# A first tile multiplied plainly, weight conversions in steps, and 12 early chunks: one change to a one-core attention and feed-forward kernel

## The chip, the core and the metric

The kernel runs on one core of one Trainium2 chip. Five engines take part, each with its own instruction stream that it works off strictly in order: TensorE (PE in the rows; its weight loads are PEld), VectorE (DVE), ScalarE (ACT), GpSimd (POOL) and SyncE (SP), which only issues transfers here. The metric is the device time of one execution in microseconds; less is better. The kernel before took 2212.39 us (median of 3 runs, 2211.89 to 2212.9).

## The reference

Channel attention, then a feed-forward network with a leaky activation. B = 4, N = 6080, C = 256, d_ff = 2048.

```python
qn = q / (np.linalg.norm(q, axis=1, keepdims=True) + 1e-06)
kn = k / (np.linalg.norm(k, axis=1, keepdims=True) + 1e-06)
s = kn.transpose(0, 2, 1) @ qn / tau          # 256 x 256 for each batch
s = s - s.max(-1, keepdims=True)
a = np.exp(s)
a /= a.sum(-1, keepdims=True) + 1e-09
x = v @ a                                     # then all batches as one list of 24320 tokens
h = x @ w_in                                  # 256 -> 2048
g = np.maximum(0.01 * h, h)
out = g @ w_out                               # 2048 -> 256
```

q, k and v are float32; w_in and w_out come as float64.

## The kernel before, in words

**The algebra.** For each batch the kernel computes the 256x256 attention matrix `a`, multiplies it into w_in once (W = a·w_in) and then needs only two products for each token: h = v·W and out = g·w_out. Every factor is kept as a high half (rounded to the fast float32 format of TensorE) and a low half (the rest), and a product is three passes: high·high, low·high, high·low.

**Batch matrices.** q and k come in 48 chunks of 128 rows, two chunks to a group. Batch 0 is worked off at the start in plain float32: ACT squares a group, DVE adds the squares up, PE multiplies (each plain float32 matmul shows as two records, so a chunk is 4 records of 256 columns). The chunks of the next batch are cast and multiplied in three passes (6 matmuls of 256 columns) in the gaps of the main loop. Batch 1 is an exception: its first FILL = 12 groups (24 chunks) are multiplied plainly during the start, where TensorE would wait for the norms, the softmax and the turn of `a`; only their squares are left for the loop ("quick" chunks).

**The main loop.** 24 tiles of 1024 tokens (6 for each batch, the last of a batch 960), and for each tile 8 pairs `p` of channel blocks: 192 steps, numbered w. In each pair h = v·W is a product of 2x2 blocks by Strassen's method (Winograd's form): 7 block products of 3 matmuls of 512 columns, `block_product`, into the PSUM banks x, y and z. ACT copies an intermediate out of its bank (`taken`), DVE adds the other bank (`add`), and `leaky` makes of each of the four results C11, C22, C21, C12 a `g_split` tile: ACT Prelu, ACT cast (high half), DVE subtract (low half). `ffn_out` then issues 24 matmuls of g·w_out, one pair later, in portions (`out(5)`, `out(5)`, `out(8)`, the rest).

**Weights.** w_in and w_out are converted from float64 words by ACT and DVE, 512 columns a block (`f64_split`, L320: two ACT steps, five DVE steps, an ACT cast for the high half, a DVE subtract for the low half). Half of w_in is converted during the chunks of batch 0, the rest and w_out in `convert` steps at the head of pairs 0 to 5. For each of 4 column groups j, `w_product` (12 matmuls for its two halves h) makes W, and `w_parts` makes of it Strassen's 7 block factors, their high and low halves, for two pairs. They go to `w_dram` and are read again for each tile (`w_load`); for batch 0 the halves are made on the tile `w_split` itself, and the whole tile is stored.

**What sets the order.** Three things. The program order, written out in the main loop. Queues (`todo`): `put` appends an entry with an estimated length to the queue of an engine, and `slot(queue, room)` at a fixed place of a pair takes entries from its head as long as they fit. And `in_order`, which ties an instruction behind the last one of its engine that was issued this way; what is not tied (the conversions, the plain products of the chunks, the chain of the start) is placed by a scheduler that follows its own estimate of time. Buffers rotate by tag: w_split 4, v_split 10, g_split 5, temp 8, raw 4 (loads of float64 words, of q and k, and of w_in halves), w_first and w_rest 1 each.

Of the kernel before, what the change touches and what calls it, by code (L numbers as in the profile page):

```python
# [11 lines left out]
I32 = mybir.dt.int32  # L12
# [9 lines left out]
EARLY_LOAD = (12, 14, 16, 18)  # L22
EARLY_SPLIT = (17, 19, 21, 23)
FILL = 12
# [7 lines left out]
def channel_attention_ffn(  # L32
# [287 lines left out]
    def f64_split(raw, hi, lo):  # L320
        low, high = raw[:, :, 0], raw[:, :, 1]
        scale, x = temp(I32, "f64_scale"), temp(I32, "f64_x")
        nc.vector.tensor_scalar(
            out=scale, in0=high, scalar1=20, scalar2=0x7FF, op0=ALU.logical_shift_right, op1=ALU.bitwise_and
        )
        nc.vector.tensor_scalar(out=x, in0=high, scalar1=0xFFFFF, scalar2=None, op0=ALU.bitwise_and)
        nc.scalar.activation(out=scale, in_=scale, func=AF.Relu, bias=exp_bias[:, 0:1], scale=2.0**23)
        tail = low.bitcast(F32)
        nc.scalar.activation(out=tail, in_=low.bitcast(U32), func=AF.Copy, scale=2.0**-52)
        nc.vector.scalar_tensor_tensor(  # L330
            out=scale, in0=high, scalar=-(2**31), in1=scale, op0=ALU.bitwise_and, op1=ALU.bitwise_or
        )
        x32 = x.bitcast(F32)
        nc.vector.scalar_tensor_tensor(out=x32, in0=x, scalar=2.0**-20, in1=tail, op0=ALU.mult, op1=ALU.add)  # L334
        nc.vector.scalar_tensor_tensor(
            out=x32, in0=x32, scalar=1.0, in1=scale.bitcast(F32), op0=ALU.add, op1=ALU.mult
        )
        nc.scalar.copy(out=hi, in_=x32)
        nc.vector.tensor_tensor(out=lo, in0=x32, in1=f32(hi), op=ALU.subtract)

    class Conversions:


        def __init__(self, blocks):
            self.blocks, self.loaded = list(blocks), []

        def load(self):
            bits, split = self.blocks.pop(0)
            self.loaded.append((f64_load(bits), split))
# [9 lines left out]
    def win_tile(early):  # L359
        if early:  # L360
            return work.tile([P, 2, TW], F32R, name="win_early", tag="v_split", bufs=VBUFS)
        return ld.tile([P, 2, TW], F32R, name="win", tag="raw", bufs=RBUFS)
# [4 lines left out]
    def win_block(j, h, early):  # L367
        def split(raw):
            w = win[j, h] = win_tile(early)
            f64_split(raw, w[:, 0, :], w[:, 1, :])  # L370
            nc.sync.dma_start(out=win_dram[j][h], in_=flat(w))

        return w_in[h * P:(h + 1) * P, j * TW:(j + 1) * TW], split

    def win_load(j):
        for h in range(CH):
            win[j, h] = win_tile(False)
            nc.sync.dma_start(out=flat(win[j, h]), in_=win_dram[j][h])
# [16 lines left out]
    def w_product(b, j, h, tag):  # L395
# [8 lines left out]
        return last  # L404

# [11 lines left out]
    def w_parts(b, j):  # L417
# [25 lines left out]
        for k in range(2):  # L443
            p, w = 2 * j + k, []

            def blocks(x0, n, name, k=k, w=w, p=p):

                if b == 0:
                    return [w_split[0, p][:, x, x0:x0 + n, :] for x in range(2)]
                w.append(work.tile([P, 2, n, P], F32R, name=name, bufs=1))  # L450
                return [w[-1][:, x] for x in range(2)]

            def store(x0, n, w=w, p=p):
                if b:
                    nc.sync.dma_start(
                        out=w_dram[b, p][:, :, x0 * P:(x0 + n) * P],
                        in_=f32(w[-1].rearrange("p x s f -> p x (s f)")),
                    )

            def begin(k=k, p=p, blocks=blocks, store=store):  # L460
                if b == 0:
                    w_split[0, p] = w_tile()
# [5 lines left out]
            def rest(k=k, p=p, blocks=blocks, store=store):  # L468
                last = split(k, blocks(S1, 4, "w_rest"), S1, (s12, S1, 2), (s34, S3, 2))
                store(S1, 4)  # L470
                if b == 0:
                    w = w_split[0, p]
                    nc.sync.dma_start(
                        out=w_dram[0, p].rearrange("p x f -> p (x f)"), in_=f32(w.rearrange("p x s f -> p (x s f)"))
                    )
                return last

            yield 1.0, begin
            yield 1.2, rest
# [11 lines left out]
    def wo_block(i):  # L491
        fs = slice(i * FPB, (i + 1) * FPB)

        def split(raw):
            f64_split(raw, *(wo[x][:, fs, :].rearrange("p f d -> p (f d)") for x in range(2)))

        return w_out.rearrange("(f p) d -> p f d", p=P)[:, fs, :], split
# [22 lines left out]
    def v_parts(i):  # L520
# [4 lines left out]
        t2 = temp(name="v_t2")[:, 0:w]  # L525
# [4 lines left out]
        yield 1.1, lambda: v_split_of(i, "B11", b11)  # L530
        yield 1.1, lambda: v_split_of(i, "B21", b21)
# [4 lines left out]
        yield 1.1, lambda: v_split_of(i, "T2", t2)  # L536
        yield 1.1, lambda: v_split_of(i, "T1", b11)
# [382 lines left out]
```

## Time and profile before

| what | value |
|---|---|
| time, median of 3 runs | 2212.39 us |
| profiled execution: time, span | 2212.01 us, 2210.1 us |
| PE busy, share of the span | 2169.7 us, 98% |
| DVE busy, ACT busy | 1472.3 us (67%), 1487.3 us (67%) |
| PE busy 0 to 50 us (chunks of batch 0) | 45.02 us |
| PE busy 50 to 85.5 us (norms, softmax, early chunks) | 29.29 us of 35.5 |
| PE busy 85.5 to 203 us (first tile) | 95.60 us of 117.5, granted clock 0.93 |
| PE busy 203 to 300 us (second tile) | 97.00 us of 97.0, granted clock 1.00 |

Rows of a timeline give the start, the time from first start to last end, engine, line, operation, tiles written and read, shape and count; in square brackets stands the idle time of the engine before, and what ended it. Rows of a group give the count, the total busy time and the mean of one in ns. A matmul's record is longer than its turn: records overlap, so the turn is read from the starts.

### The profile page before, as it was taken

The page shows a single profiled execution, that of the slowest core. Times are in us where ns is not written, and L with a number is a line of the kernel's source. Part 1 is how long each engine was busy: PE and PEld are TensorE (multiplying, and loading weights), DVE is VectorE, ACT ScalarE, POOL GpSimd, SP SyncE. Part 2 cuts the span into 40 slices and gives each one's busy share as a digit, 9 for nine tenths or more (in the row PEclk, how much of TensorE's full clock was granted, in tenths as well). Part 3 has the DMA queues.
Part 4 walks back from the last instruction along what each step waited for, and adds up shares of the span by engine and source line. Part 5 has one row for each costly group of instructions (what it writes and reads, how often), then busy time and mean ns, then how long its engine had stood idle before and what let it go on. Part 6 is the DMA issues. An engine that isn't in the chain of part 4 may idle for free.

```text
span 2210.1 us, 27204 instructions
## 1 busy us (share of the span) xinstructions
PE 2169.7 (98%) x9912; PEld 1811.7 (82%) x9912; DVE 1472.3 (67%) x2598; ACT 1487.3 (67%) x2588; POOL 3.3 (0%) x11
## 2 busy tenths in 40 slices
PE   8879999999999999999999999999999999999999
PEld 7657888888888888888888888888888888888887
DVE  7776777666776676666766767667577655556554
ACT  6567777766667777776656777777666666666665
POOL 0000000000000000000000000000000000000000
PEclk9989999999999999999999999999999999999999
DMA  9536454343753444434464344344364432333331
GB/s 360 202 143 210 152 185 146 123 137 107 238 203 115 141 145 136 160 113 140 158 221 163 131 140 158 109 158 139 103 205 146 162 123 87 135 122 104 116 119 35
DMA packets 102581, 330.89 MB, mean 150 GB/s; under 512 B 10672, under 2 KB 22832, under 8 KB 102448
## 3 DMA queue, kind: packets, MB, share of 16 engines
q1 hardware_dynamic: 102448, 329.16, 43.4%
q8 instruction: 78, 1.28, 0.2%
q14 instruction: 55, 0.45, 0.1%
HBM read 270.66 MB, written 58.46 MB: 149 GB/s over the span
## 4 chain that ended last, share of the span: by engine, by line
PE 90%; DVE 5%; DMA 3%; ACT 2%; issue 0%; SPq 0%; DVEq 0%; ACTq 0%
PE ps_o L597 44%; PE ps_x L551 22%; PE ps_z L551 11%; PE ps_y L551 6%; PE ps_s L180 4%; PE ps_s L401 2%; DVE h L572 1%; DMA qk_raw<-in_q_dram 1%; DVE g_split L565 1%; ACT g_split L563 1%; DMA qk_raw<-in_k_dram 1%; ACT h L562 1%; DMA w_dram<-w_rest 1%; DMA f_raw<-in_w_out_dram 0%; DVE f_x L334 0%
## 5 line engine op out<-in xcount | busy, mean ns | idle before, releaser
L597 PE MATMUL ps_o<-g_split,w_out_split 128*128 128x512 f32 (+1 forms) x4608 | 1164.5, 388 | 0.0
L597 PEld LDWEIGHTS ps_o<-g_split,w_out_split 128*128 128x128 f32 x4608 | 866.9, 188 | 175.3
L565 DVE TENSOR_TENSOR g_split<-h,g_split 128x512 fp32r<-128x512 f32 (+1 forms) x768 | 525.3, 684 | 399.2 <-ACT g_split L563 397.1
L551 PE MATMUL ps_x<-v_split,w_split 128*128 128x512 f32 (+1 forms) x2304 | 651.0, 390 | 21.3 <-ACT h L578 10.5
L562 ACT ACTIVATE h<-h 128x512 f32<-128x512 f32 (+1 forms) x576 | 361.9, 628 | 285.3 <-DVE h L572 285.3
L578 ACT COPY h<-ps_x 128x512 f32<-128x512 f32 (+1 forms) x576 | 334.3, 580 | 303.1 <-PE ps_x L551 302.5
L551 PEld LDWEIGHTS ps_x<-v_split,w_split 128*128 128x128 f32 x2304 | 423.3, 189 | 105.2 <-ACT h L578 16.4
L563 ACT CAST g_split<-h 128x512 fp32r<-128x512 f32 (+1 forms) x768 | 473.5, 616 | 24.0
L572 DVE TENSOR_TENSOR h<-ps_z,h 128x512 f32<-128x512 f32 (+1 forms) x384 | 262.0, 682 | 277.6 <-ACT h L578 270.3
L551 PE MATMUL ps_z<-v_split,w_split 128*128 128x512 f32 (+1 forms) x1152 | 322.8, 388 | 3.4 <-DVE h L572 3.4
L551 PEld LDWEIGHTS ps_z<-v_split,w_split 128*128 128x128 f32 x1152 | 215.7, 188 | 49.3 <-DVE h L572 5.3
L551 PE MATMUL ps_y<-v_split,w_split 128*128 128x512 f32 (+1 forms) x576 | 162.3, 390 | 0.6 <-ACT w_a L411 0.6
L572 DVE TENSOR_TENSOR h<-ps_y,h 128x512 f32<-128x512 f32 (+1 forms) x192 | 131.3, 684 | 5.2 <-PE ps_y L551 4.3
L551 PEld LDWEIGHTS ps_y<-v_split,w_split 128*128 128x128 f32 x576 | 108.6, 189 | 23.3 <-ACT w_a L411 1.1
L562 ACT ACTIVATE h<-ps_x 128x512 f32<-128x512 f32 (+1 forms) x192 | 112.8, 588 | 11.3 <-PE ps_x L551 11.3
L180 PEld LDWEIGHTS ps_s<-qk_split 128*128 128x128 f32 x720 | 102.2, 190 | 10.2 <-issue 1.0
L180 PE MATMUL ps_s<-qk_split 128*128 128x256 f32 x720 | 105.9, 283 | 0.0
L516 DVE TENSOR_TENSOR v_split<-v_raw,v_split 128x512 fp32r<-128x512 f32 (+1 forms) x144 | 98.7, 686 | 4.7
L153 DVE TENSOR_TENSOR sq_acc<-sq_acc,sq 128x512 f32<-128x512 f32 x141 | 96.2, 682 | 0.0
L158 ACT CAST qk_split<-qk_raw 128x512 fp32r<-128x512 f32 x120 | 74.2, 619 | 31.4 <-PE ps_s L180 27.5
L150 ACT ACTIVATE sq<-qk_raw 128x512 f32<-128x512 f32 x141 | 88.9, 634 | 0.0
L162 DVE TENSOR_TENSOR qk_split<-qk_raw,qk_split 128x512 fp32r<-128x512 f32 x120 | 82.1, 684 | 2.3 <-ACT qk_split L158 2.3
(106 smaller groups left out, 754.5 us busy)
## 6 DMA issues: line engine op xcount, KB each, us to landing
w_split<-w_dram SPq DMA_DIRECT2D x184, 896.0 KB, 4.7
qk_raw<-in_q_dram SPq DMA_DIRECT2D x92, 256.0 KB, 3.1
qk_raw<-in_k_dram SPq DMA_DIRECT2D x92, 256.0 KB, 3.5
v_raw<-in_vT_dram SPq DMA_DIRECT2D x40, 512.0 KB, 5.1
out_dram<-o_sb SPq DMA_DIRECT2D x80, 256.0 KB, 3.6
win<-win_dram SPq DMA_DIRECT2D x24, 512.0 KB, 4.3
w_dram<-w_rest SPq DMA_DIRECT2D x24, 512.0 KB, 3.1
w_dram<-w_first SPq DMA_DIRECT2D x24, 384.0 KB, 3.1
```

Source lines behind the costliest of these rows:

```text
L150: return nc.scalar.activation(out=out, in_=self.chunk(j), func=AF.Square)
L153: return nc.vector.tensor_tensor(out=self.acc[0], in0=self.acc[0], in1=sq, op=ALU.add)
L162: return nc.vector.tensor_tensor(out=sp[:, :, 1, :], in0=self.chunk(j), in1=f32(sp[:, :, 0, :]), op=ALU.subtract)
L180: mm = nc.tensor.matmul(out=s, lhsT=lhsT, rhs=rhs, start=False, stop=last and n == len(passes) - 1, skip_group_check=True,)
L516: last = nc.vector.tensor_tensor(out=sp[:, 1, 0:w], in0=src, in1=f32(sp[:, 0, 0:w]), op=ALU.subtract)
L551: mm = nc.tensor.matmul(out=ps[:, 0:n], lhsT=w[:, x, a, :], rhs=sp[:, y, 0:n], start=first and k == 0, stop=k == 2, skip_group_check=True,)
L562: nc.scalar.activation(out=out[:, 0:n], in_=h[:, 0:n], func=AF.Prelu, alpha=0.01)
L563: issued["act"] = nc.scalar.copy(out=sp[:, 0, 0:n], in_=out[:, 0:n])
L565: issued["dve"] = nc.vector.tensor_tensor(out=sp[:, 1, 0:n], in0=out[:, 0:n], in1=f32(sp[:, 0, 0:n]), op=ALU.subtract)
L572: issued["dve"] = nc.vector.tensor_tensor(out=h[:, 0:n], in0=ps[:, 0:n], in1=h[:, 0:n], op=ALU.add)
L578: issued["act"] = nc.scalar.copy(out=h[:, 0:n], in_=ps[:, 0:n])
L597: issued["pe"] = nc.tensor.matmul(out=o_ps[i][j][h][:, 0:n], lhsT=wo[x][:, f, h * P:(h + 1) * P], rhs=sp[:, y, 0:n], start=p == 0 and earl ...
```

## The change

Three parts, all of them before the second tile, except for the chunks.

**The first tile by the plain product.** For tile 0 the four results are computed as 2x2 blocks without Strassen's sums: `direct_product` issues 6 matmuls for each (8 blocks of 3 passes, 24 a pair instead of 21), and the results come ready in their bank, so `taken` and `add` are gone there. The factors are the halves of W as `w_product` leaves them: `direct_high` casts from PSUM on ACT, `direct_low` subtracts on DVE, into two `w_split` buffers for each j. Strassen's factors of batch 0 are now needed from tile 1 on: `direct_store` stores the three that are blocks of W straight from these halves; the four sums are made by `direct_sum` and `w_parts`' `rest` in DVE entries of length 0.9 (for batch 0 with the cast on ACT), through the one `w_rest` buffer, and stored from there.

**Conversions in steps.** `f64_split` becomes seven steps that are entries of the queues, in the fixed order; each puts the next when it is issued. The mantissa is masked and joined in place on the loaded words rather than in a temporary. w_in's first half is loaded and converted earlier in the chunks of batch 0.

**12 early chunks.** FILL goes from 12 groups to 6. The chain of the start is written out in order for PE too, with early chunks between its steps. The other 12 chunks are cast, multiplied and squared in the main loop.

```diff
-EARLY_LOAD = (12, 14, 16, 18)
-EARLY_SPLIT = (17, 19, 21, 23)
-FILL = 12
+EARLY_LOAD = (3, 7, 11, 15)
+EARLY_SPLIT = (7, 11, 15, 19)
+FILL = 6
...
-    def f64_split(raw, hi, lo):
+    def f64_steps(raw, halves, done=None):
...
+        def signed():
+            nc.vector.scalar_tensor_tensor(
+                out=to[0], in0=high, scalar=-(2**31), in1=to[0], op0=ALU.bitwise_and, op1=ALU.bitwise_or
+            )
+            return nc.vector.tensor_scalar(out=high, in0=high, scalar1=0xFFFFF, scalar2=None, op0=ALU.bitwise_and)
+
+        def joined():
+            nc.vector.scalar_tensor_tensor(out=x32, in0=high, scalar=2.0**-20, in1=tail, op0=ALU.mult, op1=ALU.add)
+            return nc.vector.scalar_tensor_tensor(
+                out=x32, in0=x32, scalar=1.0, in1=to.pop().bitcast(F32), op0=ALU.add, op1=ALU.mult
+            )
...
+        return [("dve", 0.45, exponent), ("act", 0.7, scaled), ("act", 0.7, tailed), ("dve", 1.1, signed),
+                ("dve", 1.4, joined), ("act", 0.65, high_part), ("dve", 0.7, low_part)]
...
+    WIN_HOME = ("w_split", "w_split", "v_split", "qk_split")
...
+    def direct_high(j, h):
+
+        w = w_flat()
+        w_direct[j, h] = w[:, 0:TW], w[:, TW + P:2 * TW + P]
+        return nc.scalar.copy(out=w_direct[j, h][0], in_=a_sb[0, j, h])
...
-            def blocks(x0, n, name, k=k, w=w, p=p):
-
-                if b == 0:
-                    return [w_split[0, p][:, x, x0:x0 + n, :] for x in range(2)]
+            def blocks(x0, n, name, w=w):
+
                 w.append(work.tile([P, 2, n, P], F32R, name=name, bufs=1))
                 return [w[-1][:, x] for x in range(2)]
...
-            yield 1.0, begin
-            yield 1.2, rest
+            if b:
+                yield 1.0, begin
+            yield 1.2 if b else 0.9, rest
...
+    def w_early(j, h):
...
+        def high():
+            ins = direct_high(j, h)
+            with in_order("dve"):
+                issued["dve"] = direct_low(j, h)
+            if h + 1 < CH:
+                w_early(j, h + 1)
+            return ins
...
+    def steps_work(rank, steps, then=()):
+        (engine, length, fn), *rest = steps
+        put(engine, length, fn, [("call", steps_work, rank, rest, then)] if rest else then, rank)
...
+            if i == 0:
+                for tag, (name, x, y), n in zip("xyzx", BLOCKS, (5, 5, 8, 24)):
+                    ps = bank(tag)
+                    direct_product(p, ps, x, y)
+                    slot("act", 1.4)
+                    out(n)
+                    late["bank"] = "z" if tag == "x" else "y"
+                    slot("pe_late", 0 if n == 5 else 1)
+                    leaky(i, p, name, ps, temp(name="h"))
+                    slot("act", 0.7)
+                    slot("dve", 2.6)
+                outs.append(ffn_out(i, p))
+                continue
```

What the built program makes of it is shown at two places. First PE between the last chunk of batch 0 (L180 into ps_o) and the first block product of tile 0; ps_s takes the early chunks, ps_y and ps_z the norms (L200, L254) and W (L401, now L421). Before:

```order
L200 MATMUL ps_y<-ones,sq_acc_126 128x1 x4
L254 MATMUL ps_y<-diag,ones 128x128 x2
L171 MATMUL ps_s<-qk_fill,zeros 128x512
L180 MATMUL ps_s<-qk_fill 128x256 x12
L297 MATMUL ps_x<-ident,s_sb 128x128 x4
L180 MATMUL ps_s<-qk_fill 128x256 x11
L401 MATMUL ps_y<-win_early,aT 128x512 x6
L401 MATMUL ps_z<-win_early,aT 128x512 x6
L180 MATMUL ps_s<-qk_fill 128x256 x25
L551 MATMUL ps_x<-v_split,w_split 128x512 x3
```

and now:

```order
L171 MATMUL ps_s<-qk_fill,zeros 128x512
L180 MATMUL ps_s<-qk_fill 128x256 x2
L200 MATMUL ps_y<-ones,sq_acc_126 128x1 x4
L180 MATMUL ps_s<-qk_fill 128x256 x10
L254 MATMUL ps_y<-diag,ones 128x128 x2
L180 MATMUL ps_s<-qk_fill 128x256 x8
L297 MATMUL ps_x<-ident,s_sb 128x128 x4
L180 MATMUL ps_s<-qk_fill 128x256 x2
L421 MATMUL ps_y<-w_split,aT 128x512 x6
L421 MATMUL ps_z<-w_split,aT 128x512 x6
L180 MATMUL ps_s<-qk_fill 128x256 x2
L606 MATMUL ps_x<-v_split,w_split 128x512 x6
```

A chunk is two of these instructions. Between the norms and W stand 10 chunks, as against 11 and a half before, and behind W one rather than 12 and a half.

Then ACT in the second pair of tile 0, from the Prelu of C21 to that of C12 (L562, now L617), with the semaphores each row waits for (DMAHW: a transfer). Before, where w_split are Strassen's factors of the next two pairs and f64 the conversions:

```order
L562 ACTIVATE h_838<-ps_x_768 128x512 [waits PE_49]
L563 CAST g_split_839<-h_838 128x512 [waits Activation_49]
L411 COPY w_a_843<-ps_y_820 128x512
L439 CAST w_split_851<-w_a_732 128x128
L439 CAST w_split_861<-w_a_732 128x128
L327 ACTIVATE f64_scale_886<-f64_scale_886,exp_bias_79 128x512 [waits DVE_49]
L327 ACTIVATE f64_scale_897<-f64_scale_897,exp_bias_79 128x512 [waits DVE_49]
L439 CAST w_split_851<-w_a_843 128x256 [waits Activation_49]
L439 CAST w_split_861<-w_a_843 128x256
L562 ACTIVATE h_796<-h_796 128x512 [waits DVE_49]
```

and now, where w_rest are the sums of the first two pairs' factors and win_early a converted block:

```order
L617 ACTIVATE h_772<-ps_z_757 128x512 [waits PE_49]
L618 CAST g_split_773<-h_772 128x512 [waits PE_49,Activation_49]
L489 CAST w_rest_745<-w_s_693 128x256 [waits DVE_49]
L489 CAST w_rest_745<-w_s_694 128x256 [waits DVE_49]
L489 CAST w_rest_751<-w_s_693 128x256 [waits DMAHW5_49,DVE_49]
L489 CAST w_rest_751<-w_s_694 128x256
L352 CAST win_early_790<-f64_raw_454 128x512 [waits DVE_49]
L552 CAST v_split_1167<-v_raw_586 128x512 [waits DMAHW7_49]
L552 CAST v_split_1170<-v_raw_586 128x512 [waits DMAHW0_49]
L333 ACTIVATE f64_scale_779<-f64_scale_779,exp_bias_79 128x512 [waits DVE_49]
L617 ACTIVATE h_799<-ps_x_783 128x512 [waits PE_49]
```

The second `w_rest` now waits for a transfer, the store of the first from the same buffer; eight rows stand ahead of the Prelu of C12 where seven stood, and they now wait for that transfer and for a conversion's DVE steps.

More of the change, by code (lines that the diff above doesn't have):

```diff
@@ L364, in flat, with win_tile, win_store @@
+    def win_tile(tag="raw"):
+        if tag == "raw":
+            return ld.tile([P, 2, TW], F32R, name="win", tag="raw", bufs=RBUFS)
+        if tag == "w_split":
+            return w_flat()[:, 0:2 * TW].rearrange("p (x f) -> p x f", x=2)
+        bufs = {"v_split": VBUFS, "qk_split": 3}[tag]
+        return work.tile([P, 2, TW], F32R, name="win_early", tag=tag, bufs=bufs)
     def flat(w):
         return f32(w.rearrange("p x f -> p (x f)"))
[L367 to L373, printed above, removed]
+    def win_store(j, h):
+        return nc.sync.dma_start(out=win_dram[j][h], in_=flat(win[j, h]))
@@ L453, in store, with begin @@
             def store(x0, n, w=w, p=p):
[L454 to L462, printed above, removed]
+                nc.sync.dma_start(
+                    out=w_dram[b, p][:, :, x0 * P:(x0 + n) * P], in_=f32(w[-1].rearrange("p x s f -> p x (s f)"))
+                )
+            def begin(k=k, blocks=blocks, store=store):
                 x0 = min(A11, A22)
@@ L581, in channel_attention_ffn @@
     o_ps = {}
+    BLOCKS = (("C11", 0, 0), ("C22", 1, 1), ("C21", 1, 0), ("C12", 0, 1))
     def ffn_out(i, p):
@@ L640, in run @@
             return ins
-        (todo[queue].appendleft if first else todo[queue].append)((length, run))
+        rank = 0 if first is True else first or 99
+        at = 0 if first is True else sum(x[2] <= rank for x in todo[queue])
+        todo[queue].insert(at, (length, run, rank))
     scores = [Scores(b, [G] * (NCHUNK // G)) for b in range(B)]
@@ L800, in channel_attention_ffn @@
         if i in EARLY_SPLIT:
-            conv.split()
+            for _, _, fn in early.pop(0):
+                fn()
+    for i in range(FILL):
+        with tc.issue_after(after["load"].ins):
+            raw = work.tile([P, 2, G, C], F32, name="qk_fill", tag="v_split", bufs=VBUFS)
+            after["load"] = nxt.load(i, raw)
+            if i == 1:
+                v_load(0)
+            if i == 3:
+                convert_load()
+    with tc.issue_after(after["load"].ins):
+        convert_load(4)
+        for j in range(2):
+            for h in range(CH):
+                win_store(j, h)
@@ L802, in channel_attention_ffn, with ordered @@
     filled = []
+    def ordered(engine, *fns):
+        for fn in fns:
+            with in_order(engine):
+                issued[engine] = fn()
     def fill(n):
[L805 to L816 removed]
+        for j in range(len(filled), min(len(filled) + n, FILL * G)):
+            ordered("pe", lambda: nxt.product(j))
+            filled.append(j)
```

254 lines of the change are left out of this document (144 added, 110 removed).

## The prediction

> **What bounds the kernel now.** I read the busy time by stretches first. The first row is the chunks of batch 0, the next two are the first and the second tile (columns: stretch, its length, PE, PEld, DVE, ACT, POOL busy with counts, granted clock, DMA share, GB/s); then, from PE's timeline, the starts of tile 1 and of its second pair.
>
> ```profile
> 0.00:50.00 50.00, 45.02 (x194) 38.26 (x194) 38.24 (x49) 35.73 (x41) 1.76 (x8) 1.00 0.97 358
> ...
> 85.50:203.00 117.50, 95.60 (x376) 73.01 (x375) 87.60 (x169) 76.55 (x145) 0.52 (x1) 0.93 0.43 151
> 203.00:300.00 97.00, 97.00 (x430) 80.32 (x429) 69.02 (x111) 75.80 (x133) 0.00 (x0) 1.00 0.58 198
> ...
> 202.98 0.84 PE L551 MATMUL ps_x<-v_split,w_split 128*128 128x512 f32 x3
> ...
> 213.18 0.84 PE L551 MATMUL ps_x<-v_split,w_split 128*128 128x512 f32 x3
> ```
>
> From tile 1 on TensorE never waits: a pair of 45 matmuls takes 10.20 us, 0.2267 us each. There only the count of matmuls matters. Tile 0 is another stage: it issues 8x21 block products, 7x24 out matmuls and 36 for W, 372 in all or 84.3 us, and lasts from 85.59 to 202.98, 117.4 us. So 33.1 us are lost there. Two views say to what: the waits of PE in that stretch (total, times, longest), and the rows around the longest waits.
>
> ```profile
> PE ps_x L551 <- ACT h L578: 10.5, 7, 5.0
> PE ps_x L551 <- DVE w_split L440: 10.2, 3, 4.7
> ...
> 114.18 1.22 PE L551 MATMUL ps_x<-v_split,w_split 128*128 128x512 f32 x2 [4.74 <-DVE w_split L440]
> ...
> 118.38 0.86 PE L551 MATMUL ps_x<-v_split,w_split 128*128 128x512 f32 x3
> ...
> 157.34 1.65 PE L551 MATMUL ps_x<-v_split,w_split 128*128 128x512 f32 x3 [5.04 <-ACT h L578]
> ...
> 163.72 0.86 PE L551 MATMUL ps_x<-v_split,w_split 128*128 128x512 f32 x3
> ```
>
> TensorE waits for ACT and DVE, which wait for each other over conversions and factors. The restart costs too: from 114.18 to 118.38 stand 10 matmuls (2.3 us) in 4.2, from 157.34 to 163.72 17 of them (3.9) in 6.4: 1.9 and 2.5 us behind waits of 4.7 and 5.0, none visible behind waits near 1.
>
> **The start: 18.0 us less.** PE's timeline before the first block product, and the DVE rows that close the steps of the chain (rest of the norms, row maximum, normed):
>
> ```profile
> 5.67 43.19 PE L180 MATMUL ps_o<-qk_raw 128*128 128x256 f32 x192
> 52.62 1.34 PE L200 MATMUL ps_y<-ones,sq_acc 128*128 128x1 f32 x8 [3.77 <-DVE sq_acc L191]
> 57.55 1.19 PE L254 MATMUL ps_y<-diag,ones 128*128 128x128 f32 x4 [3.59 <-DVE diag L246]
> 58.53 1.92 PE L171 MATMUL ps_s<-qk_fill,zeros 128*128 128x512 f32 x2
> 60.24 6.95 PE L180 MATMUL ps_s<-qk_fill 128*128 128x256 f32 x24
> 67.03 0.60 PE L297 MATMUL ps_x<-ident,s_sb 128*128 128x128 f32 x4
> ...
> 72.03 1.74 PE L401 MATMUL ps_y<-win_early,aT 128*128 128x512 f32 x6
> 73.60 1.54 PE L401 MATMUL ps_z<-win_early,aT 128*128 128x512 f32 x6
> 74.98 10.95 PE L180 MATMUL ps_s<-qk_fill 128*128 128x256 f32 x50
> 85.59 1.05 PE L551 MATMUL ps_x<-v_split,w_split 128*128 128x512 f32 x3
> ...
> 57.12 0.48 DVE L246 TENSOR_SCALAR diag<-ident,rn 128x128 f32<-128x128 f32 x2
> 62.40 0.62 DVE L288 TENSOR_SCALAR s_sb<-s_sb,den 128x256 f32<-128x256 f32 x2
> ```
>
> The plain products still end at 48.9. A plain chunk is 4 records; 50 records in 10.6 us make 0.85 us a chunk. Zeros (1.7) and one chunk lead to 51.4, where the norms start (the conversions now come before the last groups, so DVE's sums end at about that time, not at 52.6). From norms to normed DVE needed 52.62 to 63.0, 10.4 us; now PE's five chunks (4.3) are 0.7 longer than DVE's steps up to diag (54.0 to 57.6): 62.5. The turn is no longer behind chunks (before it stood at 67.03, four late): aT is whole at 64.5, W's 12 matmuls end at 66.8, the last chunk at 67.6. The first block product starts at 67.6 as against 85.59.
>
> **Matmuls: 5.4 more and 8.6 more.** Tile 0 has 24 matmuls more, 24 x 0.2267 = 5.4 us. The 12 chunks come back into the loop with 6 matmuls each:
>
> ```profile
> 332.58 0.88 PE L180 MATMUL ps_s<-qk_split 128*128 128x256 f32 x6
> 333.30 0.86 PE L551 MATMUL ps_x<-v_split,w_split 128*128 128x512 f32 x3
> ```
>
> 0.72 us a chunk, 8.6 us for 12, in a stretch where PE is never idle, so nothing hides them. Their casts and subtracts go beside it: 36 chunks over 22 pairs now, 24 over 15 before, 1.6 a pair either way. I take nothing for them; if that cover is gone, one ACT cast in each of 12 pairs could be late, 12 x 0.6 = 7 us.
>
> **Waits in tile 0: 33.1 before, 39.6 now.** I followed the built order row by row through tile 0, with these means and 0.05 us from an engine to the next.
>
> ```profile
> L563 ACT CAST g_split<-h 128x512 fp32r<-128x512 f32 x640 | 397.4, 621 | 20.0
> L562 ACT ACTIVATE h<-ps_x 128x512 f32<-128x512 f32 x160 | 94.8, 592 | 11.3 <-PE ps_x L551 11.3
> L565 DVE TENSOR_TENSOR g_split<-h,g_split 128x512 fp32r<-128x512 f32 x640 | 441.4, 690 | 340.1 <-ACT g_split L563 338.0 <-DMA v_raw<-in_vT_dram 1.3
> L326 DVE TENSOR_SCALAR f_x<-f_raw 128x512 int32<-128x512 int32 x16 | 6.8, 423 | 0.0
> L334 DVE SCALAR_TENSOR_TENSOR f_x<-f_x,f_raw 128x512 f32<-128x512 int32 x16 | 10.9, 687 | 0.2
> ...
> 26.76 0.69 DVE L330 SCALAR_TENSOR_TENSOR f_scale<-f_raw,f_scale 128x512 int32<-128x512 int32 x1
> 27.49 0.69 DVE L335 SCALAR_TENSOR_TENSOR f_x<-f_x,f_scale 128x512 f32<-128x512 f32 x1
> ```
>
> A DVE step that needs the one before starts 0.73 after it (26.76, 27.49). A step in a slot costs more than its length: behind a block's cast DVE does the low half (0.6), then `signed` and `joined` (0.7+0.5+0.7+0.7), 3.3 us in all, and the conversion's high half stands on ACT *ahead* of the next Prelu. From Prelu to Prelu such a block takes 0.67+0.62+3.3+0.57 = 5.2 us; PE needs 10.9/4 = 2.7 for it. ACT falls 2.5 behind at each of eleven conversions and catches up in blocks without (1.2). PE feels it where a bank comes back soon: C12 and the next C11 both use x, and W's halves take y and z. The sums, by the pair whose start or inside is late:
>
> - pair 0: W's second low half stands behind four conversion steps (2.7); y waits for C22's Prelu (1.7), z for C21's (3.0), x for C12's (2.3): 9.7.
> - into pair 2: `w_rest`, below: 9.9, restart 2.5. Inside it 0.5.
> - pair 3: out waits for the w_out block that is just being converted (1.3), then x for C12 (2.8): 4.1.
> - pair 4: `w_rest` again: z (2.5) and x (6.0), restart 2: 10.5.
> - pair 5: x behind the last conversions: 2.3. Pairs 6 and 7: none.
>
> The price of `w_rest` has a row: one buffer, two writers in a row. Before, in a later batch:
>
> ```profile
> 641.30 0.75 DVE L440 TENSOR_TENSOR w_rest<-w_s,w_rest 128x256 fp32r<-128x256 f32 x2
> 646.20 0.50 DVE L439 CAST w_rest<-w_s 128x256 fp32r<-128x256 f32 x2 [2.30 <-DMA w_dram<-w_rest]
> ```
>
> From the last write (642.05) to the next 4.15 us. There DVE alone waited and PE had other work. Now the cast is ACT's, so ACT stands still with the Prelu of C12 behind it. In pair 1: C21's cast ends at 93.6, the sums are ready at 95.4, the first pair's halves at 96.3, the store is through at 100.5, the second's halves take to 101.3, then a conversion's high half waits for two DVE steps (103.7), two casts for tile 1 and a step (105.8), Prelu (106.5). PE has run out of work at 96.6: 9.9 us. Bounds for this wait: 2.3 as in the row, if ACT and DVE are far ahead, and 12 if steps in place are slower. I keep 9.9, since DVE is behind, not ahead, at that point.
>
> One price no row has: the mask (L342) now writes in place, every second word. L326 (423 ns) is its nearest row, L334 (687) the upper bound; I take 423, and 11 x 0.26 = 3 us more is kept for the range. The Trainium skill, VectorE: DVE Perf Modes, section What auto-detection actually checks, says that an operation of one source gets its doubled rate from where its operands lie and from even outer sizes; by that rule a stride changes nothing, and the sum stays. No run here shows it yet.
>
> The Trainium skill, DMA: Bandwidth & Descriptors, section Anatomy of one DMA, fits a transfer by 2.0 us and bytes at 436 GB/s, for transfers from another queue than this one: 512 KB would take an estimated 3.2 us, and the sum would be about 3 us lower over three stores. The measured row decides, with 4.15.
>
> **Tile 1, first pair: 8.5.** The fourth group's `w_rest` pair falls between C11's copy and its Prelu. ACT's next copy, which frees x, comes 11 us after the pair's start (copy, square, casts, 4.15 for the store, casts, add, Prelu, cast); PE has 22 matmuls, 5.0 us, until then, so 6 to 7, and 1.5 to 2.5 of restart. I take 8.5.
>
> **The sum.** -18.0 + 5.4 + 8.6 + (39.6 - 33.1) + 8.5 = +11.0 us on a span of 2210.1, so 2221.1; the profiled execution has 1.9 us around its span and lies 0.4 under the median: 2223.4. In short, time = 2212.4 + (W - 37.1), where W is all that PE loses between the first product and the second pair of tile 1; I have W = 48.1.
>
> **Rivals.**
>
> *The steps come in time: faster.* The fixed order may spread the steps so that ACT is ahead when a store is waited for; then each of the three stores costs the row's 2.3 and no restart, the ping-pong of pairs 3 to 5 falls to 3, pair 0 stays: W = 9.7 + 7 + 3 = 20, time 2195. For it: DVE has 87.6 us and ACT 76.6 us of work in tile 0 before, and the change takes 24 copies and 24 adds away there, so neither engine is full. Against: these are waits of one engine for another in order, which average load does not remove (before, with the same load, 33 us were lost). It decides from W under 32.7. 25%.
>
> *It cancels.* W between 32.7 and 41.5, within 0.2% (4.4 us), about what a measurement of this kernel can tell from no change: only one of the three stores is felt in full. 2212. 17%.
>
> *As forecast, or worse: slower.* W over 41.5. At its far end the in-place steps are slow (3), casts are late in the loop (7): 2233. 58%.
>
> *The start is not shorter.* The first halves of W are written over buffers of w_in halves whose store must be through; those stores stand in SP's queue behind early chunks and two loads. At the 358 GB/s of the first 50 us, 512 KB in 1.5 us, they end near 63, before W's product at 66.8; if 5 us later, the time is 3 us more. Part of the last case.
>
> So 2223, with 2200 to 2234 for eight in ten; the likeliest case's own range is 2217 to 2234. Faster 0.25, same 0.17, slower 0.58.
>
> **What would show it.** Right: PE's first L606 row at 67 to 69; waits of PE for ACT's Prelu (L617) at a pair's start, and of ACT's `w_rest` cast for the transfer, three or four of about 4 us; tile 1 starting at 195 to 200; a wait in its first pair; all else as before plus 8.6 us. Wrong: tile 1 starting before 185, or waits of PE from 300 us on.

## The result: 0.7% slower

The changed kernel takes 2226.83 us (median of 6 runs, 2224.09 to 2230.09) against 2212.14 us (6 runs, 2211.48 to 2213.22): ratio 1.0067, 95% interval 1.0054 to 1.0080. The forecast was 2223, slower, with 2200 to 2234 around it.

The profiled execution of the changed kernel took 2228.81 us, 2.0 more than the median, with a span of 2227.0. It is taken apart at the same places as before. First the busy time by stretches (length, then PE, PEld, DVE, ACT and POOL busy with counts, granted clock, DMA share, GB/s): tile 0, and the first pair of tile 1.

```profile
66.68:196.26 129.58, 103.77 (x398) 80.67 (x397) 84.83 (x153) 69.15 (x124) 0.52 (x1) 0.89 0.41 134
196.26:217.42 21.16, 12.12 (x47) 9.57 (x45) 8.79 (x18) 9.85 (x20) 0.00 (x0) 0.76 0.71 247
```

| term | predicted | measured, us |
|---|---|---|
| start, to the first block product | -18.0 | 66.68 - 85.59 = -18.9 |
| tile 0 (5.4 of matmuls, 6.5 of waits) | +11.9 | 129.6 - 117.4 = +12.2 |
| first pair of tile 1 | +8.5 | 21.2 - 10.2 = +11.0 |
| the rest, up to the end of the span | +8.6 | 2009.6 - 1996.9 = +12.7 |
| sum, on the span | +11.0 | 2227.0 - 2210.1 = +16.9 |

Then PE's timeline of the changed kernel: the first block product, the three longest waits of tile 0 (the last value in brackets is what ended the wait), the start of tile 1 and the wait in its first pair.

```profile
66.68 1.62 PE L606 MATMUL ps_x<-v_split,w_split 128*128 128x512 f32 x4
...
81.39 2.93 PE L421 MATMUL ps_z<-w_split,aT 128*128 128x512 f32 x6 [2.58 <-ACT h L617]
...
106.18 2.93 PE L606 MATMUL ps_x<-v_split,w_split 128*128 128x512 f32 x6 [7.10 <-ACT h L617]
108.91 2.33 PE L653 MATMUL ps_o<-g_split,w_out_split 128*128 128x512 f32 x5
...
159.51 2.93 PE L606 MATMUL ps_x<-v_split,w_split 128*128 128x512 f32 x6 [4.62 <-ACT h L617]
...
196.26 0.84 PE L593 MATMUL ps_x<-v_split,w_split 128*128 128x512 f32 x3
...
210.46 1.65 PE L593 MATMUL ps_x<-v_split,w_split 128*128 128x512 f32 x3 [9.04 <-ACT h L633]
```

TensorE stands where the prediction put the waits: for the Prelu of C12 ahead of pair 2 and inside pair 4, and for a copy in the first pair of tile 1. What holds ACT there is read from ACT's own timeline, in pair 1 and in the first pair of tile 1:

```profile
95.75 0.71 ACT L489 CAST w_rest<-w_s 128x256 fp32r<-128x256 f32 x2
100.15 0.71 ACT L489 CAST w_rest<-w_s 128x256 fp32r<-128x256 f32 x2 [3.70 <-DMA w_dram<-w_rest]
103.32 0.67 ACT L352 CAST win_early<-f_raw 128x512 fp32r<-128x512 f32 x1 [2.46 <-DVE f_raw L346]
103.89 1.14 ACT L552 CAST v_split<-v_raw 128x512 fp32r<-128x512 f32 x2
104.93 0.72 ACT L333 ACTIVATE f_scale<-f_scale,exp_bias 128x512 int32<-128x512 int32 x1
105.55 0.58 ACT L617 ACTIVATE h<-ps_x 128x512 f32<-128x512 f32 x1
...
198.16 0.70 ACT L489 CAST w_rest<-w_s 128x256 fp32r<-128x256 f32 x2
206.81 0.71 ACT L489 CAST w_rest<-w_s 128x256 fp32r<-128x256 f32 x2 [7.95 <-DMA w_dram<-w_rest]
```

In the 9.8 us from 95.75 to 105.55 ACT waits 6.2: first for the store of `w_rest`, then, with the Prelu still behind it, for DVE's steps of a conversion. In tile 1 the store alone holds it 7.95 us.

### The profile page after: what moved, and what is told of

It is laid out like the page before. It is cut to its first block, busy times and chain, and to the rows that moved or that the text cites. A ratio compares the mean times of both kernels' runs of the same rounds, so it can differ in the third digit from the quotient of the medians.

```text
span 2227.0 us, 27287 instructions
## 1 busy us (share of the span) xinstructions
PE 2177.6 (98%) x9960; PEld 1819.0 (82%) x9960; DVE 1464.8 (66%) x2572; ACT 1479.1 (66%) x2564; POOL 3.3 (0%) x11
## 4 chain that ended last, share of the span: by engine, by line
PE 90%; DVE 4%; DMA 2%; ACT 2%; issue 1%; SPq 0%; ACTq 0%; DVEq 0%
PE ps_o L653 44%; PE ps_x L593 22%; PE ps_z L593 11%; PE ps_y L593 5%; PE ps_s L180 4%; PE ps_s L421 1%; DMA w_dram<-w_rest 1%; ACT h L617 1%; DVE g_split L620 1%; ACT g_split L618 1%; PE ps_x L606 1%; DVE h L627 1%; DMA qk_raw<-in_k_dram 1%; DVE sq_acc L140 0%; DVE w_rest L490 0%
## 5 line engine op out<-in xcount | busy, mean ns | idle before, releaser
L593 PE MATMUL ps_x<-v_split,w_split 128*128 128x512 f32 (+1 forms) x2208 | 621.3, 390 | 9.0 <-ACT h L633 9.0
L617 ACT ACTIVATE h<-h 128x512 f32<-128x512 f32 (+1 forms) x552 | 346.7, 628 | 273.8 <-DVE h L627 273.8
L633 ACT COPY h<-ps_x 128x512 f32<-128x512 f32 (+1 forms) x552 | 320.8, 581 | 280.3 <-PE ps_x L593 279.7
L593 PEld LDWEIGHTS ps_x<-v_split,w_split 128*128 128x128 f32 x2208 | 405.5, 189 | 83.1 <-ACT h L633 11.1
L627 DVE TENSOR_TENSOR h<-ps_z,h 128x512 f32<-128x512 f32 (+1 forms) x368 | 250.9, 682 | 262.4 <-ACT h L633 259.0
L593 PE MATMUL ps_z<-v_split,w_split 128*128 128x512 f32 (+1 forms) x1104 | 309.4, 388 | 5.7 <-DVE h L627 5.7
L593 PEld LDWEIGHTS ps_z<-v_split,w_split 128*128 128x128 f32 x1104 | 206.7, 188 | 49.7 <-DVE h L627 7.6
L617 ACT ACTIVATE h<-ps_x 128x512 f32<-128x512 f32 (+1 forms) x200 | 117.8, 589 | 11.9 <-PE ps_x L606 8.2
L180 PEld LDWEIGHTS ps_s<-qk_split 128*128 128x128 f32 x792 | 112.4, 190 | 11.1 <-issue 1.0
L593 PEld LDWEIGHTS ps_y<-v_split,w_split 128*128 128x128 f32 x552 | 103.8, 188 | 21.1 <-issue 0.5
L180 PE MATMUL ps_s<-qk_split 128*128 128x256 f32 x792 | 116.4, 283 | 0.0
L162 DVE TENSOR_TENSOR qk_split<-qk_raw,qk_split 128x512 fp32r<-128x512 f32 x132 | 90.3, 684 | 4.7 <-ACT qk_split L158 4.7
```

The lines of the kernel that those rows point to most:

```text
L162: return nc.vector.tensor_tensor(out=sp[:, :, 1, :], in0=self.chunk(j), in1=f32(sp[:, :, 0, :]), op=ALU.subtract)
L180: mm = nc.tensor.matmul(out=s, lhsT=lhsT, rhs=rhs, start=False, stop=last and n == len(passes) - 1, skip_group_check=True,)
L593: mm = nc.tensor.matmul(out=ps[:, 0:n], lhsT=w[:, x, a, :], rhs=sp[:, y, 0:n], start=first and k == 0, stop=k == 2, skip_group_check=True,)
L617: nc.scalar.activation(out=out[:, 0:n], in_=h[:, 0:n], func=AF.Prelu, alpha=0.01)
L627: issued["dve"] = nc.vector.tensor_tensor(out=h[:, 0:n], in0=ps[:, 0:n], in1=h[:, 0:n], op=ALU.add)
L633: issued["act"] = nc.scalar.copy(out=h[:, 0:n], in_=ps[:, 0:n])
```

## The experiments

All kernels compute the whole reference. Each is compared with the kernel before, run beside it; the ratio is to that. The first four start from the changed kernel.

**1. No factor waits for a store.** Of batch 0, the second pair of a group of factors goes to two other buffers.

```diff
             def rest(k=k, blocks=blocks, store=store):
+                if b == 0 and k == 1:
+                    first = work.tile([P, 2, 3, P], F32R, name="w_first", bufs=1)[:, :, 0:2, :]
+                    other = temp(F32R, "w_other").rearrange("p (x s f) -> p x s f", x=2, f=P)
+                    for of, x0, src in ((first, S1, s12), (other, S3, s34)):
+                        last = split(k, [of[:, x] for x in range(2)], x0, (src, x0, 2))
+                        w.append(of)
+                        store(x0, 2)
+                    return last
```

> Batch 0's second pair of each group of factors is written to two other buffers (two blocks each, with a store each), so that no factor waits for a store. Theory (the one buffer and its store are what ACT stands for, 3.7, 4.4 and 8.0 us in three of the four groups): TensorE's waits at 106.2, 159.5 and 210.5 us (7.1, 1.3 + 4.6 and 9.0) shrink by about 3.5, 4.4 and 7, and with them restarts of the clock of about 0.5, 1.4 and 2: 17 to 19 us in all, 2208 to 2211. Rival (the conversions alternate between ACT and DVE and would hold ACT there anyway): the wait goes to the next conversion's high half, and no more than a third is won: 2219 to 2223.

Measured: 2210.8 us (10 runs, 2207.98 to 2214.59), ratio 0.9994 (0.9985 to 1.0003): 16 us less than the changed kernel, no difference from the kernel before. PE's row ahead of pair 2 and the stretch of the first pair of tile 1:

```profile
104.04 2.41 PE L614 MATMUL ps_x<-v_split,w_split 128*128 128x512 f32 x6 [3.73 <-ACT h L625]
...
189.61:200.01 10.40, 10.40 (x46) 8.37 (x45) 6.35 (x12) 8.78 (x18) 0.00 (x0) 1.00 1.01 364
```

The 7.10 became 3.73, the 1.31 and 4.62 in pair 4 became one wait of 2.65, and the first pair of tile 1 has no wait left (10.40 us against 21.16). The theory holds, at the slow end of its 2208 to 2211: without the waits for the stores the change would have cost nothing. Inside tile 0 the loss is still 30.8 us (120.6 long, 89.8 of matmuls), so another cause stays.

**2. The casts on DVE.** Buffer and store stay, DVE writes both halves.

```diff
-                (nc.vector.tensor_copy if b else nc.scalar.copy)(out=hi, in_=src)
+                nc.vector.tensor_copy(out=hi, in_=src)
```

> Batch 0's factors are cast on DVE (as in the later batches) instead of on ACT; buffer, store and order stay. Theory (the store holds whoever writes the buffer next, and since ACT and DVE need each other's steps, the other one is held a step later): the three waits move from ACT to DVE and TensorE wins at most the ACT casts themselves, 0 to 6 us: 2221 to 2227. Rival (it is only ACT standing ahead of a Prelu that hurts, as in the later batches, where DVE waits and TensorE does not): 10 to 17 us less, 2210 to 2217.

Measured: 2224.65 us (4 runs, 2224.45 to 2226.72), ratio 1.0061 (1.0045 to 1.0078). DVE's waits from 66 to 218 us (total, times, longest), and PE's two longest:

```profile
DVE w_rest L489 <- DMA w_dram<-w_rest: 17.5, 4, 7.0
...
104.99 2.92 PE L606 MATMUL ps_x<-v_split,w_split 128*128 128x512 f32 x6 [6.72 <-ACT h L617]
...
208.17 1.65 PE L593 MATMUL ps_x<-v_split,w_split 128*128 128x512 f32 x3 [8.22 <-ACT h L633]
```

As the theory had it: now DVE stands 17.5 us for the store, ACT needs DVE's steps, and TensorE waits 6.72 and 8.22 us where it waited 7.10 and 9.04. It is the buffer, not the engine that writes it.

**3. The Prelu first.** In tile 0 ACT's queue entries go behind the Prelu and cast of their block.

```diff
-                    slot("act", 1.4)
                     out(n)
                     ...
                     leaky(i, p, name, ps, temp(name="h"))
+                    slot("act", 1.4)
                     slot("act", 0.7)
```

> In tile 0 the step of a conversion or of W's halves that ACT takes in a block goes behind that block's Prelu and cast, not ahead of them; nothing else is changed. Theory (a conversion's high half on ACT, ahead of the Prelu, waits 2.1 to 3.4 us for three DVE steps, and TensorE feels it where a bank comes back): the waits at 81.4, 86.3, 137.7, 159.5 and 174.4 us (2.6, 1.9, 2.5, 4.6, 2.1) lose 1.5 to 2.5 each and the one at 106.2 loses 2: 10 to 13 us less, 2214 to 2217; the waits of ACT for the store stay. Rival (the stores alone make the loss, the alternation costs TensorE nothing): within 3 us of 2227.

Measured: 2203.06 us (7 runs, 2198.58 to 2209.41), ratio 0.9959 (0.9947 to 0.9972): 24 us less than the changed kernel, twice the theory's 10 to 13. What ACT waits for between 66 and 218 us (total, times, longest), first in the changed kernel, then here; behind them PE's wait ahead of pair 2 here:

```profile
ACT w_out_split L352 <- DVE f_raw L346: 21.6, 8, 3.4
ACT w_rest L489 <- DMA w_dram<-w_rest: 16.1, 3, 7.9
ACT win_early L352 <- DVE f_raw L346: 7.8, 3, 2.7
```

```profile
ACT w_rest L489 <- DMA w_dram<-w_rest: 16.2, 3, 7.9
...
ACT w_out_split L352 <- DVE f_raw L346: 4.9, 4, 2.8
ACT win_early L352 <- DVE f_raw L346: 1.7, 2, 1.3
```

```profile
98.35 2.93 PE L606 MATMUL ps_x<-v_split,w_split 128*128 128x512 f32 x6 [2.36 <-ACT h L617]
```

ACT waits for the stores as long as before, but 29.4 us of waiting for DVE's steps became 6.6. Tile 0 goes from 129.6 to 105.3 us (the profile is of the slowest of the seven runs, whose first product came 3.1 us later than in the changed kernel's). Of these 24.3 us, 16.2 are waits, and 8.1 are matmuls that are busy 95.7 us instead of 103.8. The theory counted waits alone; most of the 8.1 is TensorE's clock, which stands at 0.50 for two windows of 3.41 us in tile 0 here and for eight in the changed kernel. Of the waits, the one in pair 1 shrank more than forecast: in the changed kernel 5.4 us lie between the end of the wait for the store (100.15) and the Prelu (105.55); with the Prelu first it follows the casts, and TensorE's wait falls from 7.10 to 2.36, by 4.7 where 2 was forecast, though the store takes as long. The wait in tile 1 stays at 9.0, as the edit is in tile 0 alone.

**4. Both edits.**

> The edits of the two other buffers and of the Prelu first together. Theory (two separate causes): the gains add, 27 to 32 us less, 2195 to 2200, faster than the kernel before. Rival (both shorten the same waits): no more than 3 us below the better of the two alone.

Measured: 2185.83 us (4 runs, 2184.2 to 2189.6), ratio 0.9885 (0.9870 to 0.9900): faster than both kernels. The gains add, 16.0 + 23.8 alone and 41.0 together; the theory's count of two causes holds, its 2195 to 2200 was too high by what the third run won more. Tile 0 and the first pair of tile 1, and all that PE still waits for in them:

```profile
66.44:166.19 99.75, 94.92 (x399) 76.44 (x398) 86.95 (x158) 69.09 (x126) 0.52 (x1) 0.97 0.56 181
166.19:176.58 10.39, 10.39 (x47) 8.37 (x45) 6.35 (x12) 8.78 (x18) 0.00 (x0) 1.00 1.01 355
...
PE ps_x L614 <- DVE w_split L437: 2.2, 1, 2.2
PE ps_x L614 <- ACT h L625: 2.1, 1, 2.1
PE ps_o L661 <- DVE w_out_split L355: 0.5, 2, 0.3
```

So the plain first tile, the steps and the 12 chunks need not cost anything: 41 us lay in one buffer and in the place of one queue slot. What each of the three parts gains by itself was not measured, except for the chunks, on the kernel before.

**5. The 12 chunks alone**, on the kernel before.

```diff
-FILL = 12
+FILL = 6
...
-        quick = 10 if done else 0
+        quick = 3 if done else 0
...
-            at(max(w0, when[i * G] - 3), lambda sc=sc, i=i: sc.load(i, qk_raw()))
+            at(max(w0 + (NPAIR - 2 if b == 1 else 0), when[i * G] - 3), lambda sc=sc, i=i: sc.load(i, qk_raw()))
```

> One part of the change alone, on the kernel before: 12 early chunks instead of 24 (with the two bounds on when the later chunks are loaded and squared), the first tile still by Strassen's method and the conversions as before. It takes 24 of the 50 matmul rows out of the stretch from 74.98 to 85.59 us. Theory (in the kernel before these chunks cover DVE's conversions, sums and factors, which end at 79 to 83 us, so that without them TensorE waits): the first block product starts at 79.5 to 81 instead of 85.6, with 1 to 3 us of waits and of the low clock behind it, and the 12 chunks cost 12 x 0.72 = 8.6 in the loop: slower by 4 to 8 us, 2216 to 2220. Rival (nothing but TensorE's own work stands in the start): the start is 12 x 0.85 = 10.2 shorter, 1.6 us faster, 2210 to 2211.

Measured: 2221.07 us (5 runs, 2217.56 to 2222.65), ratio 1.0037 (1.0024 to 1.0050), just above the theory's range. PE's timeline at the start of tile 0:

```profile
75.24 0.58 PE L551 MATMUL ps_x<-v_split,w_split 128*128 128x512 f32 x1
79.19 0.80 PE L551 MATMUL ps_x<-v_split,w_split 128*128 128x512 f32 x2 [3.36 <-DVE w_split L440]
79.78 1.49 PE L551 MATMUL ps_y<-v_split,w_split 128*128 128x512 f32 x3
...
85.60 0.96 PE L551 MATMUL ps_x<-v_split,w_split 128*128 128x512 f32 x3 [2.03 <-ACT h L578]
```

The first product could go at 75.2, 10.3 us earlier, but the low half of its factor comes from DVE at 79, behind the conversions and sums, and the clock is low afterwards: tile 1 starts at 198.86 instead of 202.98. So 10.2 us of chunks taken away gave 4.1 back, and they cost 10.6 in the rest of the span. In the changed kernel the first product starts at 66.7, as soon as TensorE's own work allows, and a wait of 2.15 us for W's second low half follows at 70.46. That this start is so early because the plain first tile needs no sums is argued here; no run tests it by itself.

**6. W's second low half first**, on the kernel with both edits: `direct_low` of both halves goes ahead of `wo_first[3]` and `wo_first[4]`.

```diff
-        ordered("dve", (parts[3], wo_first[4])[h], lambda: direct_low(0, h))
-        if h == 0:
-            ordered("dve", wo_first[3])
+        ordered("dve", *([parts[3]] if h == 0 else []), lambda: direct_low(0, h))
+    ordered("dve", wo_first[3], wo_first[4])
```

> The kernel with both edits, and the low half of W's second product goes ahead of four DVE rows of the first conversion at the start of tile 0 (they come right behind it). Theory (the 2.15 us that TensorE waits for that low half are only its place in DVE's order): this wait goes, the one for the bank of C12 in the same pair (2.05) stays or grows by up to 1, since the conversion's high half comes as late as before: 1 to 2 us less than with both edits, 2183 to 2185. Rival (DVE's work is needed in pair 0 anyway): the same time as with both edits, and the 2.15 turn up at the next wait.

Measured: 2187.06 us (4 runs, 2185.5 to 2188.96), ratio 0.9886 (0.9872 to 0.9901). Not told apart from run 4. In the profile the wait of 2.15 is gone, 0.57 came at W's next product and 2.13 stayed at C12, and tile 0 is 96.0 us long instead of 99.8; but the first product starts at 68.8 instead of 66.4, because TensorE's wait for the sums of squares was 1.15 us here (none in the profile of run 4) and the clock was low behind it, 0.60 from 53 to 57 us. The edit is worth less than this scatter.

**7. 16 early chunks**, on the kernel with both edits.

```diff
-FILL = 6
+FILL = 8
```

> The kernel with both edits, and 16 early chunks instead of 12, the four more all between W and the first block product. Theory (a chunk in the loop costs its whole 0.72 us; four chunks ahead of the first product cost 4 x 0.85 = 3.4, of which they cover the 2.15 us wait for W's second low half): 1.3 in the start against 2.9 in the loop, 1.6 us less than with both edits, 2183 to 2185. Rival (the later chunks cost little, something else made the loop longer): 1 to 3 us more, 2187 to 2189.

Measured: 2184.03 us (4 runs, 2184.01 to 2184.26), ratio 0.9873 (0.9856 to 0.9889), the lowest median of the study. It is 1.8 less than run 4 where 1.6 was expected, but the intervals overlap, so the two are not told apart. The profile follows the theory at the start: the first product at 70.38 instead of 66.44 (3.9 later), and the wait for W's second low half is gone; tile 0 takes 95.4 instead of 99.8.

**8 and 9. The wait for the sums of squares.** Between profiles of kernels whose start is the same, the first block product moved by up to 3.4 us (66.44 in run 4, 69.82 in run 3, about 1 us of it from late loads of batch 0). The rows at the norms' products (L200) suggested why, so the wait there was taken away in one kernel and made longer in another. The first has both edits, 16 chunks, the low half first and

```diff
-    fill(1)
+    fill(2)
     ordered("pe", sc.norms_mm)
     ordered("dve", sc.norms_taken, sc.norms_begun, sc.norms)
-    fill(5)
+    fill(4)
```

> Both edits, 16 early chunks, W's second low half ahead of the conversion's rows, and two chunks instead of one ahead of the norms' products (one fewer behind them), so that TensorE has work while DVE adds up the squares. Theory (a wait of about 1 us at that place starts, in some executions, some 3.3 us at a granted clock of 0.50, which cost 1.7, and this makes the scatter between runs): no wait and no low clock between 49 and 62 us, first block product 0 to 1 us earlier than with 16 chunks alone: 2182 to 2184. Rival (the scatter comes from elsewhere): the same mean as with 16 chunks alone, 2184 to 2185, and a low clock in that stretch all the same.

and the other has no `fill` ahead of `norms_mm` and `fill(6)` behind it, with 16 chunks and both edits.

> The opposite at the same place: both edits and 16 early chunks, no chunk ahead of the norms' products, so that TensorE waits for the sums of squares 2 to 3 us instead of 0.6. The chunk and its opening product move behind them and are in the way of the chain there by 1.7 us. Theory (a wait starts a stretch at half the clock): granted clock 0.50 for 3 to 7 us between 52 and 62 us, 1.7 us or more on top: 2187 to 2190. Rival (the clock falls for another reason): 1.7 later only, 2185 to 2186.5, and full clock there.

Measured: 2184.44 us (4 runs, 2182.41 to 2185.14), ratio 0.9879 (0.9865 to 0.9894), and 2186.93 us (4 runs, 2186.18 to 2188.27), ratio 0.9894 (0.9878 to 0.9911). PE's row of the first, then rows and stretches of 1 us of the second:

```profile
51.75 0.95 PE L200 MATMUL ps_y<-ones,sq_acc 128*128 128x1 f32 x8
```

```profile
51.61 1.05 PE L200 MATMUL ps_y<-ones,sq_acc 128*128 128x1 f32 x8 [2.64 <-DVE sq_acc L191]
...
53.47 7.03 PE L180 MATMUL ps_s<-qk_fill 128*128 128x256 f32 x24
...
52.00:53.00 1.00, 1.00 (x7) 0.80 (x8) 0.27 (x2) 0.02 (x1) 0.00 (x0) 1.00 1.06 404
53.00:54.00 1.00, 1.00 (x4) 0.63 (x3) 0.83 (x6) 0.00 (x0) 0.00 (x0) 0.74 1.05 385
54.00:55.00 1.00, 1.00 (x4) 0.82 (x3) 0.83 (x6) 0.00 (x0) 0.00 (x0) 0.50 1.05 389
55.00:56.00 1.00, 1.00 (x4) 0.73 (x4) 0.86 (x6) 0.67 (x1) 0.00 (x0) 0.50 1.05 387
56.00:57.00 1.00, 1.00 (x4) 0.82 (x3) 0.90 (x3) 0.00 (x0) 0.00 (x0) 0.55 1.05 387
57.00:58.00 1.00, 1.00 (x7) 0.87 (x6) 0.00 (x0) 0.62 (x1) 0.00 (x0) 1.00 1.04 383
```

The mechanism is the theory's: a wait of 2.64 us is followed by full speed for nearly two microseconds, then by some 3.4 us at half the clock, which cost 1.7 us; the first product comes 3.45 later than in run 7 (73.83 against 70.38, 1.7 of it the moved chunk) and the time is 2.9 more than in run 7, and 2.5 more than that of the kernel without the wait, which ran beside it. Without the wait the clock stays at 1.00 from 49 to 62 us. But the time of that kernel is that of run 7, and its runs scatter by 2.7 us where those of run 7 lie within 0.3: the scatter between runs does not come from this place alone. That half of the theory fell.

## Why the prediction was right, step by step

**The start** (-18.0, measured -18.9) came out within 1 us: the first block product at 66.68 for 67.6. That the norms start at 51.34, for 51.4, is in part luck. The zeros ahead of them were priced at 1.7 us by rows of the kernel before that ran at half the clock (58.53 to 60.24); they took 0.86 (48.78 to 49.64), and a wait of 0.67 for DVE's sums filled most of the difference. That the first halves of W would wait for w_in's stores was a rival part that did not occur.

**The matmuls** (5.4) hold: tile 0 has 396 of them, 89.8 us by the row of 0.2267. **The chunks in the loop** (8.6) hold as a price: a chunk takes 0.71 us between these rows of the changed kernel, with nothing that hides it.

```profile
250.51 0.88 PE L180 MATMUL ps_s<-qk_split 128*128 128x256 f32 x6
251.22 0.86 PE L593 MATMUL ps_x<-v_split,w_split 128*128 128x512 f32 x3
```

The rest of the span grew by 12.7, and the other 4 are not chunks. Nearly all of it can be read at the ends of batches. The first row is of the kernel before (PE's waits after tile 1's first pair), the others of the changed one:

```profile
PE ps_z L551 <- DVE h L572: 3.4, 3, 1.4
```

```profile
PE ps_z L593 <- DVE h L627: 5.7, 3, 2.2
...
1738.17 0.96 PE L593 MATMUL ps_z<-v_split,w_split 128*128 128x512 f32 x3 [2.17 <-DVE h L627]
...
1740.00:1745.00 5.00, 5.00 (x17) 4.07 (x16) 3.31 (x6) 3.39 (x7) 0.00 (x0) 0.69 1.01 288
```

2.3 us more of waits, and a stretch at the low clock behind one of them (5 x 0.31 = 1.6 us). "From tile 1 on TensorE never waits" was read from 203 to 300 us and is wrong three times in the span: TensorE waits at about 648, 1186 and 1723 us in the kernel before, and at 662, 1200 and 1738 us in the changed one. So one of the prediction's own signs of being wrong, waits of PE from 300 us on, is there, though not as something new. Whether the change makes these waits longer was not tested: the experiments' profiles have 4.7 to 6.3 there (4.9 with the 12 chunks alone), the one profile of the kernel before 3.4.

**Waits in tile 0** (39.6, measured 39.8) is right as a sum by luck, and wrong in its parts: the waits were put 9.3 us too high, and the slow matmuls 9.5 us too low. The step that failed is the restart term, which the prediction sized at 4.5 us in all, from two waits of 4.7 and 5.0 us, with "none visible behind waits near 1". PE is idle 129.58 - 103.77 = 25.8 us in tile 0, where the prediction's waits come to 35.1; and its matmuls are busy 103.77 us where 89.8 are needed, 14.0 us more. About 10.9 of them are the clock, an estimate from its eight windows of 3.41 us at 0.50 in tile 0 (the last section says how they are found): TensorE is busy 21.7 us in these, and half of that is lost. What the other 3 are is not shown. The row of the kernel before, quoted in the prediction, gave the size: 95.60 busy for 84.3 of work, 11 of the 33 us (6 of them the clock, by the same estimate). The waits that came out too large are those of pair 0 (9.7 forecast; 2.15, 0.25, 2.58 and 1.94 measured), the one into pair 2 (9.9; 7.10) and those in pair 4 (8.5; 1.31 and 4.62).

**The store** was taken at 4.15 us from the last write to the next. Measured were 3.2 in pair 1 (the last write ends at 96.9, the next starts at 100.2), 4.0 in pair 4 and 7.5 in tile 1, and the last, 3.4 above the price, is enough for the 2.5 us by which **tile 1's first pair** (8.5, measured 11.0) came out longer. The transfers of the buffer, from issue to landing:

```profile
DMA to landing us min/median/max: 3.0/3.1/7.4
```

The long one is issued at 199.38, behind two loads of v and two of factors, 2.8 MB in all, issued from 194.68 on. The Trainium skill, DMA: Bandwidth & Descriptors, section Anatomy of one DMA, fits 2.0 us and 436 GB/s for transfers that GpSimd issues, an estimated 3.2 for 512 KB; the median of 3.1 for these stores, which SyncE issues, agrees, and the 7.4 shows what the fit does not include, the transfers ahead. Run 1 settles that the stores were felt in all three places, and with that the rival by which only one is felt in full fell.

**The alternation of ACT and DVE** was the right mechanism at too low a price. Moving the Prelu ahead won 24 us; the prediction had 12 for it in its list (y, z and x in pair 0, x in pairs 3 and 5) and put the 5.4 us between the store and the Prelu of pair 1 wholly down to the store. The two causes were in series there, and either edit shortens that wait. The list also holds no clock behind these waits, as above.

**The mask in place** (423 taken, 687 as bound) has its row now:

```profile
L342 DVE TENSOR_SCALAR f_raw<-f_raw 128x512 int32<-128x512 int32 x16 | 6.9, 428 | 0.5
```

428 ns in place and over every second word: by the rule of the Trainium skill, VectorE: DVE Perf Modes, section What auto-detection actually checks, a stride changes nothing for an operation of one source, and the trace agrees.

**The rivals.** That the steps come in time (2195) did not occur, and run 4 shows under what condition it does: with the store's buffer and the Prelu's place mended, W falls to 9.95 + 0.2 = 10.1 us, below that rival's 20. What spoke for it, that neither engine is full (DVE 84.8 and ACT 69.2 us of 129.6 in tile 0), was true and had no weight: what decided was the order within each engine.

## What to carry to other kernels

Where two engines take turns on one job, what stands ahead of the step that frees TensorE's bank counts, not how full the engines are: put that step first in each engine's order, and the job's steps behind it. A buffer that is written again right after its store holds whoever writes it, for the whole transfer and all transfers queued ahead; moving the write to another engine only moved the wait here. And price a wait of TensorE with its clock: compare the busy time of its matmuls with their count times their turn at full speed, stretch by stretch, as a bound (14.0 us in tile 0), and count the windows of 3.41 us at half the clock in it, up to 1.7 us each (10.9).

## What the runs showed of the hardware

TensorE's granted clock is 1.00 or 0.50 in these profiles, and it changes on a grid of 3.41 us that runs through the whole execution. In the changed kernel the stretches at 0.50 begin at 70.60, 80.84, 87.66, 101.32, 138.86, 159.34, 203.72 and 1739.71 us. These starts lie 3, 5, 9, 20, 26, 39 and 489 windows of 3.413 us behind the first, and each stretch lasts one window or three.

What decides is how busy TensorE was in the window before. The eleven profiles, read window by window from 5 to about 220 us, show this. At the full clock, a window in which PE was busy for at most 41% was followed by half the clock in 32 of 32 cases, one of 43 to 49% in three of eight. From 50% on, only four were: they hold the eight matmuls of one column at the norms' products, and are busy for 55 to 68% with these, some 28 to 41% without. At half the clock, a window busy for at most 74% was followed by another one in 18 of 18 cases, and one of 84% or more by the full clock in 39 of 39.

So the length of a wait does not say what it costs. At the norms' products, waits of 0.60, 0.67 and 1.05 us (run 7, the changed kernel, run 2) were followed by the full clock, and waits of 1.09, 1.15, 1.26 and 2.64 us (runs 3, 6, 1 and 9) by a stretch at 0.50. Run 7 and run 9 have the same work at the first C12, behind a wait of 2.05 us. In run 7 the whole wait lies in one window, which is busy for 1.36 of 3.41 us, and 9 matmuls follow in the next; in run 9 a part of the wait falls into the next window, the first is busy for 1.59, and 14 matmuls follow. The first two rows are of run 7, the others of run 9:

```profile
78.83:82.24 3.41, 1.36 (x6) 1.05 (x6) 3.38 (x7) 3.38 (x7) 0.00 (x0) 1.00 0.30 82
82.24:85.65 3.41, 3.41 (x9) 2.63 (x8) 3.38 (x7) 2.76 (x5) 0.00 (x0) 0.50 0.93 259
```

```profile
80.80:84.21 3.41, 1.59 (x8) 0.97 (x6) 3.27 (x7) 2.39 (x5) 0.00 (x0) 1.00 0.09 25
84.21:87.62 3.41, 3.18 (x14) 2.63 (x15) 3.34 (x6) 3.35 (x7) 0.00 (x0) 1.00 0.71 166
```

Where the grid lies differs from one profiled execution to the next. That this makes a part of the scatter between runs is likely, but not shown.

The Trainium skill, TensorE: Matmul & The Clock Gate, section Part 1: The HAM clock gate, speaks of a free-running window of 3.4 us and of half the clock after an idle window. The length and the free run agree with these traces. That the window must be idle does not: windows in which TensorE was busy for up to 41% of the time did it here.
